# Where the first expert slot takes its memory from, and the order of splits, a routing step and a table around it

## The chip, the cores and the metric

The kernel runs on one core of a Trainium2 chip. The metric is the device time of one execution in microseconds. Before the change three runs gave a median of 810.86 us (810.6 to 813.5). The engines of the core run their own instruction streams in order and wait for each other by semaphores: TensorE (PE), VectorE (DVE), ScalarE (ACT), GpSimd (POOL) and SyncE (SP, which only issues transfers here).

## The reference

Attention with a sigmoid in place of the softmax, and after it a mixture of experts in which every token goes to the one expert with the highest logit:

```python
q, k, v: (8, 12, 448, 64)              # batch, heads, sequence, head dim
scores = matmul(q, k^T) / 8 - log(448)
attn_out = matmul(sigmoid(scores), v)
x = attn_out.transpose(0, 2, 1, 3).reshape(3584, 768)
e_idx = argmax(x @ w_gate, axis=1)     # 8 experts
gate_w = softmax(x @ w_gate)[e_idx];   eom = sigmoid(x @ w_output_gate)
for e in range(8):
    h = maximum(x[e_idx == e] @ w1[e], 0)          # 768 -> 1024
    out[e_idx == e] = gate_w * eom[:, e] * (h @ w2[e])   # 1024 -> 768
```

## The kernel before

**Attention** (`attention`) walks 24 groups of two head pairs. PE multiplies, ACT applies the sigmoid, DVE adds the halves, transposes 32x32 blocks into `xt` (token rows of one batch, two buffers), and after the sixth pair of a batch SP writes `xt` to `x_dram`. Gate logits of four pairs at a time come from `gates`. Per batch, `route` turns logits into a place in one list per expert. It is a generator of steps, "logits", "counts", "places", "rows": after "places" POOL makes `pos`, `den` and others in a chain of small operations, and "rows" begins with DVE's reciprocal of `den` (line 274), after which POOL scatters the list entries.

**Experts.** Tokens of one expert are worked in slots of 256. The first three slots (early) are filled from the first six batches before attention ends; `table(True)` makes the plan of the late slots from all counts, in five parts on DVE, each a step. Each slot (`slot`, line 493) has this work:

- layer 1, eight blocks f of 128 hidden units: twelve matmuls (lines 458, 459) into one of three PSUM banks; then ACT copies half the sum, DVE adds the other (`gl`, line 467), and `high_low` makes the high and low part of block f - 1 in `h` (ACT 471, DVE 472);
- layer 2, four outputs (t, n): 24 matmuls each (lines 484 to 486), the high, low-weight and low-activation products of all eight blocks. ACT evicts y (line 487), POOL scatters rows of y to `out` (line 489).

All numbers are carried as a rounded high part and a low remainder. A split is a cast on ACT (line 424) and a subtraction on DVE (line 425). w2 of a slot is split in four pieces during its layer 1 (`split_w2`, before block 0 and at blocks 1, 3, 5). w1 and the tokens of the next slot are split during layer 2 of this one: three pieces of w1 (`split_w1`), and three of x after `turn_x` has transposed the gathered rows (line 443). POOL gathers the next slot's rows from `x_dram` (line 402, eight gathers), SP loads w1 and w2 only where the expert changes (line 414).

The order on each engine is the order of this code; nothing reorders it. `side()` in `build` is a generator of other work, a step of which runs after each block of layer 1 (not after block 7) and after outputs 1 to 3 of layer 2. It holds the rest of the last batch's routing (`rt`), then the five parts of the late table, then per group of lists the load from DRAM (`load_list`, SP) and, three steps later, the spread over partitions (`spread_lists`: a DVE transpose, line 386, and twelve POOL copies).

Memory of the attention comes from the pool `attn`, which is given back when attention has been issued. `late_memory` then takes its tiles from the same addresses: `h`, `y`, `hb`, `hx`, `w2h`, `w2l`, in this order. A tile there waits for the last reader or writer of what lay at its place, a transfer included.

Of the kernel before, what the change touches and what calls it, by code (L numbers as in the profile page):

```python
# [9 lines left out]
F32 = mybir.dt.float32  # L10
F32R = mybir.dt.float32r
# [3 lines left out]
ALU = mybir.AluOpType  # L15
# [5 lines left out]
B, H, S, D = 8, 12, 448, 64  # L21
NPAIR = H // 2
E = 8
DM = H * D
# [23 lines left out]
def r32(ap):  # L48
    return ap.bitcast(F32)


class Kernel:
# [48 lines left out]
    def late_memory(self):  # L101
        p = self.pool("late")
        self.hs = [p.tile([128, 8, TS], F32R, name=f"h{i}") for i in range(2)]
        self.ys = [p.tile([128, DM], F32, name=f"y{i}") for i in range(2)]
        hb = p.tile([128, DF], F32, name="hb")
        self.hb = hb
        self.hx = p.tile([128, 4, Q4], F32, name="hx")
        self.w2h = p.tile([128, 8, DM], F32R, name="w2h")
        self.w2l = [p.tile([128, 4, DM], F32R, name=f"w2l{i}") for i in range(2)]
        self.lr = [hb[0:32, 192 * i:192 * i + 192] for i in range(5)]  # L110
# [312 lines left out]
    def split(self, raw, hi, lo):  # L423
        self.nc.scalar.copy(hi, raw)  # L424
        self.nc.vector.tensor_tensor(lo, raw, r32(hi), ALU.subtract)  # L425

    def split_w1(self, k):
        self.split(self.w1r[:, 2 * k:2 * k + 2], self.w1p[0][k], self.w1p[1][k])

# [62 lines left out]

    def slot(self, cur, nxt, side=None, begun=False, drain=False):
        nx = self.load_slot(*nxt) if nxt is not None else None
        if drain:
            self.gather(dict(lx=self.lxb[:, 1], xg=self.half_x(1)))
            self.nc.gpsimd.drain()
        self.split_w2(0)
        for f in range(8):
            self.layer1(f, begun and f == 0)  # L500
            if f:
                self.high_low(f - 1)
            if f in (1, 3, 5):
                self.split_w2(f // 2 + 1)
            if side is not None and f < 7:
                next(side, None)
        self.high_low(7)
        self.load_w2(nx)
        self.turn_x(nx)
        self.split_x(nx, 0)  # L510
        self.split_x(nx, 1)
        for i, (t, n) in enumerate(((0, 0), (0, 1), (1, 0), (1, 1))):
            self.layer2(cur, t, n, self.ys[t])
            if i == 0:
                self.split_x(nx, 2)
            if i < 3 and nx is not None:
                self.split_w1(i)
            if side is not None and i > 0:
                next(side, None)
        return nx  # L520
# [59 lines left out]

    def attention(self, pool):
        nc = self.nc
# [3 lines left out]
        t = lambda n, shape: pool.tile(shape, F32, name=n)  # L586
# [6 lines left out]
        xh = t("xh", [128, S])  # L593
        xt = [t(f"xt{i}", [128, S // 32, NPAIR * 32]) for i in range(2)]
        half = [slice(0, 64), slice(64, 128)]
# [78 lines left out]
        for u in range(U * NG + LAG):  # L674
            g, i = divmod(u, U)
# [52 lines left out]
    def build(self, phases="abc"):  # L728
        tc, nc = self.tc, self.nc
# [3 lines left out]
        self.memory()  # L733
        with tc.tile_pool(name="attn", bufs=1) as p:
            rt = self.attention(p)
        self.late_memory()
# [6 lines left out]
        early = lambda k: (self.tab_e, k, self.lts[:, k], self.lxs[:, k], ROWS_E)  # L743
        late = lambda k: (self.tab_l, k, self.lts[:, EARLY + k], self.lxs[:, EARLY + k])

        def side():
# [5 lines left out]
            next(rt)  # L752
            yield
            for _ in rt:
                yield
            yield
            for _ in self.table(True):
# [28 lines left out]
        sd = side()  # L786
        self.mm_ps = self.mm_late
        cur = self.s0
        for k in range(EARLY - 1):
            cur = self.slot(cur, early(k + 1), sd, k == 0)  # L790
        cur = self.slot(cur, late(0), sd)
# [53 lines left out]
```

## Time and profile before

| what | us |
|---|---|
| median of three runs | 810.86 |
| the profiled execution | 810.35 |
| its span | 808.5 |
| PE busy | 788.5 (98%) |
| DVE busy | 503.3 (62%) |
| ACT busy | 490.9 (61%) |
| POOL busy | 311.6 (39%) |

Attention takes the first 282 us; slot 0 begins there with block 0, and slots 1, 2 and 3 begin layer 1 at about 324, 361 and 394 us. After 763 us two half slots of 128 tokens end the kernel. Where PE is at 98%, the only time that another engine can cost is where PE stands still: the timeline of PE shows it in brackets at the instruction after the stand, with the releaser. One bracket further back, the releaser's own timeline tells what that engine had waited for. Spans of POOL are rough.

### The profile page before, as it was taken

The page shows a single profiled execution, that of the slowest core. Times are in us where ns is not written, and L with a number is a line of the kernel's source. Part 1 is how long each engine was busy: PE and PEld are TensorE (multiplying, and loading weights), DVE is VectorE, ACT ScalarE, POOL GpSimd, SP SyncE. Part 2 cuts the span into 40 slices and gives each one's busy share as a digit, 9 for nine tenths or more (in the row PEclk, how much of TensorE's full clock was granted, in tenths as well). Part 3 has the DMA queues.
Part 4 walks back from the last instruction along what each step waited for, and adds up shares of the span by engine and source line. Part 5 has one row for each costly group of instructions (what it writes and reads, how often), then busy time and mean ns, then how long its engine had stood idle before and what let it go on. Part 6 is the DMA issues. An engine that isn't in the chain of part 4 may idle for free. (4 is left out here: it accounts for less than half of the span.)

```text
span 808.5 us, 15212 instructions
## 1 busy us (share of the span) xinstructions
PE 788.5 (98%) x5772; PEld 582.8 (72%) x5772; DVE 503.3 (62%) x731; ACT 490.9 (61%) x665; POOL 311.6 (39%) x454
## 2 busy tenths in 40 slices
PE   9999999999999988999999999999999999999996
PEld 4333333333333378799899999999999999999885
DVE  2344434434457656876767776767767667676696
ACT  5666666666568535464656656665566565665585
POOL 4003302310334565738445144352445523525152
PEclk9999999999999999999999999999999999999999
DMA  6353543525558320236218571192175101758371
GB/s 251 131 206 130 160 192 138 206 87 189 196 181 335 124 103 6 77 111 237 91 40 316 189 267 51 29 332 94 41 257 173 50 39 40 271 160 316 121 299 39
DMA packets 32312, 126.81 MB, mean 157 GB/s; under 512 B 5535, under 2 KB 7823, under 8 KB 28256
## 3 DMA queue, kind: packets, MB, share of 16 engines
q1 hardware_dynamic: 22288, 100.81, 35.1%
q0 software_dynamic: 9936, 24.88, 9.3%
q8 instruction: 50, 0.82, 0.4%
q14 instruction: 38, 0.31, 0.1%
HBM read 153.15 MB, written 23.64 MB: 219 GB/s over the span
## 5 line engine op out<-in xcount | busy, mean ns | idle before, releaser
L458 PE MATMUL ps<-rounded 128*128 128x512 f32 x672 | 236.9, 395 | 4.2 <-DVE gl L467 4.1
L611 ACT ACTIVATE a<-ps,bias_s 128x896 f32<-128x896 f32 x168 | 169.0, 1008 | 97.4 <-PE ps L609 97.4
L459 PE MATMUL ps<-rounded 128*128 128x256 f32 x672 | 189.0, 281 | 1.3 <-DVE rounded L425 1.3
L425 DVE TENSOR_TENSOR rounded<-plain,rounded 128x2048 fp32r<-128x2048 f32 (+3 forms) x107 | 148.9, 1413 | 49.5 <-ACT rounded L424 49.4
L402 POOL DMA_INDIRECT plain<-x_dram,lxs x120 | 149.8, 1248 | 36.6 <-issue 34.8
L486 PE MATMUL ps<-w2h,h 128*128 128x384 f32 x480 | 161.2, 336 | 2.4 <-DVE h L472 1.9
L484 PE MATMUL ps<-w2h,h 128*128 128x384 f32 x480 | 160.8, 335 | 0.3 <-ACT h L471 0.3
L485 PE MATMUL ps<-w2l,h 128*128 128x384 f32 x480 | 160.5, 334 | 0.0
L609 PE MATMUL ps<-kqv 64*64 64x448 f32 x1344 | 158.1, 541 | 0.4 <-ACT a L611 0.4
L618 PE MATMUL ps<-a,kqv 64*64 64x448 f32 x1344 | 157.1, 536 | 0.5 <-ACT pc L260 0.5
L458 PEld LDWEIGHTS ps<-rounded 128*128 128x128 f32 x672 | 126.5, 188 | 34.3 <-DVE gl L467 5.5
L424 ACT CAST rounded<-plain 128x2048 fp32r<-128x2048 f32 (+3 forms) x107 | 124.8, 1199 | 40.8 <-DVE plain L443 40.8
L425 DVE TENSOR_TENSOR w2l<-plain,w2h 128x1536 fp32r<-128x1536 f32 x62 | 108.7, 1758 | 61.1 <-ACT w2h L424 61.1
L459 PEld LDWEIGHTS ps<-rounded 128*128 128x128 f32 x672 | 127.8, 190 | 1.6 <-DVE rounded L425 1.6
L489 POOL DMA_INDIRECT out<-y,lts x28 | 51.2, 1827 | 199.2 <-ACT y L487 131.1
L466 ACT COPY gl<-ps 128x256 f32<-128x256 f32 x112 | 41.7, 373 | 110.1 <-DVE h L472 81.6
L618 PEld LDWEIGHTS ps<-a,kqv 64*64 64x64 f32 x1344 | 51.5, 133 | 76.2 <-issue 74.2
L609 PEld LDWEIGHTS ps<-kqv 64*64 64x64 f32 x1344 | 48.7, 133 | 74.1 <-issue 61.5
L424 ACT CAST w2h<-plain 128x1536 fp32r<-128x1536 f32 x62 | 90.8, 1471 | 11.2 <-DMA x_dram<-xt 8.1
L486 PEld LDWEIGHTS ps<-w2h,h 128*128 128x128 f32 x480 | 90.1, 188 | 4.4 <-DVE h L472 2.4
L484 PEld LDWEIGHTS ps<-w2h,h 128*128 128x128 f32 x480 | 90.1, 188 | 1.7 <-ACT h L471 1.0
L485 PEld LDWEIGHTS ps<-w2l,h 128*128 128x128 f32 x480 | 90.1, 188 | 0.1
(183 smaller groups left out, 563.6 us busy)
## 6 DMA issues: line engine op xcount, KB each, us to landing
plain<-w SPq DMA_DIRECT2D x68, 768.0 KB
plain<-w SPq DMA_DIRECT2D x48, 1024.0 KB
kqv<-kqv SPq DMA_DIRECT2D x23, 1344.0 KB
x_dram<-xt SPq DMA_DIRECT2D x8, 1344.0 KB
plain<-w SPq DMA_DIRECT2D x6, 512.0 KB
plain<-x_dram,lxs POOLq DMA_INDIRECT x120, 3.7
kqv<-kqv SPq DMA_DIRECT2D x1, 896.0 KB
lst<-plain POOLq DMA_DIRECT2D x1, 726.0 KB, 7.5
```

The source lines that it names most:

```text
L402: self.nc.gpsimd.indirect_dma_start(out=s["xg"][:, g], out_offset=None, in_=x4, in_offset=bass.IndirectOffsetOnAxis(ap=s["lx"][:, g:g + 1] ...
L424: self.nc.scalar.copy(hi, raw)
L425: self.nc.vector.tensor_tensor(lo, raw, r32(hi), ALU.subtract)
L458: nc.tensor.matmul(ps, wh[d][:, c], self.xc[:, d].rearrange("p a t -> p (a t)"), start=(d == 0), stop=False)
L459: nc.tensor.matmul(ps[:, 0:TS], wl[d][:, c], self.xc[:, d, 0], start=False, stop=(d == 5))
L484: nc.tensor.matmul(ps, hh[:, f, tk], wh, start=(f == 0), stop=False)
L485: nc.tensor.matmul(ps, hh[:, f, tk], wl, start=False, stop=False)
L486: nc.tensor.matmul(ps, hl[:, f, tk], wh, start=False, stop=(f == 7))
L489: nc.gpsimd.indirect_dma_start(out=self.out, out_offset=bass.IndirectOffsetOnAxis(ap=s["lt"][:, t, 0:1], axis=0), in_=y, in_offset=None, b ...
L609: nc.tensor.matmul(ps[half[h], j, 0:S], kg[half[j], e, 0, o:o + 64], kg[half[j], e, 1], start=True, stop=True)
L611: nc.scalar.activation(at[u % 4], ps[:, :, 0:S], AF.Sigmoid, bias=self.bias_s, scale=1.0 / math.sqrt(D))
L618: nc.tensor.matmul(self.ps_o[e][h][half[j], 0:S], v[half[h], 6 if i == 3 else 3 * e + c, j], a[half[h], j], start=(i in ((0, 3 if h else 4 ...
```

## The change

The rows' tiles `xt` come from a second pool, `rows`. The late tiles are divided: `h`, `w2h` and half of `w2l` from the first pool, the rest, `w2l1`, `y`, `hb`, `hx`, from a pool behind it. In `slot`, w1's first piece is split in two: its cast ahead of `turn_x`, its subtraction behind all three token splits; the other two pieces follow outputs 0 and 1 instead of 1 and 2. In slot 0 a step of `side` runs also after block 7; the routing's "rows" step moves there from block 6, and the table's first part moves from output 2 to output 1 of layer 2. So all later steps come one step sooner.

```diff
     def late_memory(self):
         p = self.pool("late")
         self.hs = [p.tile([128, 8, TS], F32R, name=f"h{i}") for i in range(2)]
+        self.w2h = p.tile([128, 8, DM], F32R, name="w2h")
+        w2l = p.tile([128, 4, DM], F32R, name="w2l0")
+        p = self.pool("later")
+        self.w2l = [w2l, p.tile([128, 4, DM], F32R, name="w2l1")]
         self.ys = [p.tile([128, DM], F32, name=f"y{i}") for i in range(2)]
...
-        self.w2h = p.tile([128, 8, DM], F32R, name="w2h")
-        self.w2l = [p.tile([128, 4, DM], F32R, name=f"w2l{i}") for i in range(2)]
...
+    def high_w1(self, k):
+        self.nc.scalar.copy(self.w1p[0][k], self.w1r[:, 2 * k:2 * k + 2])
+
+    def low_w1(self, k):
+        self.nc.vector.tensor_tensor(self.w1p[1][k], self.w1r[:, 2 * k:2 * k + 2], r32(self.w1p[0][k]), ALU.subtract)
+
     def split_w1(self, k):
-        self.split(self.w1r[:, 2 * k:2 * k + 2], self.w1p[0][k], self.w1p[1][k])
+        self.high_w1(k)
+        self.low_w1(k)
...
-    def slot(self, cur, nxt, side=None, begun=False, drain=False):
+    def slot(self, cur, nxt, side=None, begun=False, drain=False, steps=7):
...
-            if side is not None and f < 7:
+            if side is not None and f < steps:
                 next(side, None)
         self.high_low(7)
         self.load_w2(nx)
-        self.turn_x(nx)
-        self.split_x(nx, 0)
-        self.split_x(nx, 1)
+        if nx is not None:
+            self.high_w1(0)
+            self.turn_x(nx)
+            for k in range(3):
+                self.split_x(nx, k)
+            self.low_w1(0)
         for i, (t, n) in enumerate(((0, 0), (0, 1), (1, 0), (1, 1))):
             self.layer2(cur, t, n, self.ys[t])
-            if i == 0:
-                self.split_x(nx, 2)
-            if i < 3 and nx is not None:
-                self.split_w1(i)
+            if i < 2 and nx is not None:
+                self.split_w1(i + 1)
...
-        xt = [t(f"xt{i}", [128, S // 32, NPAIR * 32]) for i in range(2)]
+        xt = [rows.tile([128, S // 32, NPAIR * 32], F32, name=f"xt{i}") for i in range(2)]
...
-        with tc.tile_pool(name="attn", bufs=1) as p:
-            rt = self.attention(p)
+        with tc.tile_pool(name="attn", bufs=1) as p, tc.tile_pool(name="rows", bufs=1) as q:
+            rt = self.attention(p, q)
...
             yield
             next(rt)
             yield
+            next(rt)
+            yield
+            yield
             for _ in rt:
                 yield
-            yield
             for _ in self.table(True):
                 yield
...
-            cur = self.slot(cur, early(k + 1), sd, k == 0)
+            cur = self.slot(cur, early(k + 1), sd, k == 0, steps=8 if k == 0 else 7)
```

DVE at the end of slot 0's layer 1, before: `gl` is a block's sum, the operation into `h` a block's low half (the last two stand in one row), `den` the routing's.

```order
L261 RECIPROCAL sg<-sg 112x32
L467 TENSOR_TENSOR gl_113<-gl_113,ps 128x256
L472 SCALAR_TENSOR_TENSOR h_2441<-gl_113,h_2440 128x256
L274 RECIPROCAL den<-den 112x4
L467 TENSOR_TENSOR gl_113<-gl_113,ps 128x256
L472 SCALAR_TENSOR_TENSOR h_2441<-gl_113,h_2440 128x256 x2
L443 STREAM_TRANSPOSE plain<-plain 128x8x6x32
```

The same place after:

```order
L263 RECIPROCAL sg<-sg 112x32
L476 TENSOR_TENSOR gl_113<-gl_113,ps 128x256
L481 SCALAR_TENSOR_TENSOR h_2445<-gl_113,h_2444 128x256
L476 TENSOR_TENSOR gl_113<-gl_113,ps 128x256
L481 SCALAR_TENSOR_TENSOR h_2445<-gl_113,h_2444 128x256
L276 RECIPROCAL den<-den 112x4
L481 SCALAR_TENSOR_TENSOR h_2445<-gl_113,h_2444 128x256
L452 STREAM_TRANSPOSE plain<-plain 128x8x6x32
```

The sum of block 7 and the low half of block 6 now stand ahead of the reciprocal of `den`; the low half of block 7 alone stands behind it.

ACT from the end of layer 1 of a slot through its layer 2, before: `rounded` with 128x2x256 is a cast of tokens, with 128x2048 one of w1, `y` an eviction.

```order
L471 ACTIVATE h_2440<-gl_113 128x256 x2
L424 CAST rounded<-plain 128x2x256 x2
L487 ACTIVATE y_2442<-ps,lts 128x384
L424 CAST rounded<-plain 128x2x256
L424 CAST rounded<-plain 128x2048
L487 ACTIVATE y_2442<-ps,lts 128x384
L424 CAST rounded<-plain 128x2048
L487 ACTIVATE y_2443<-ps,lts 128x384
L424 CAST rounded<-plain 128x2048
L487 ACTIVATE y_2443<-ps,lts 128x384
L424 CAST w2h<-plain 128x1536
```

The same place after:

```order
L480 ACTIVATE h_2444<-gl_113 128x256 x2
L430 CAST rounded<-plain 128x2048
L426 CAST rounded<-plain 128x2x256 x3
L496 ACTIVATE y_2452<-ps,lts 128x384
L430 CAST rounded<-plain 128x2048
L496 ACTIVATE y_2452<-ps,lts 128x384
L430 CAST rounded<-plain 128x2048
L496 ACTIVATE y_2453<-ps,lts 128x384 x2
L426 CAST w2h<-plain 128x1536
```

The first cast of w1 has moved from behind the first eviction to ahead of the tokens, the other two by one output each, and the last two evictions follow each other.

## Rows read from the trace of the kernel before

**Rows 1.** The windows view: us; busy (instructions) of PE, PEld, DVE, ACT, POOL; clock, DMA, GB/s.

```profile
290.00:300.00 10.00, 7.66 (x41) 6.57 (x42) 7.38 (x15) 4.84 (x10) 8.01 (x7) 0.83 0.19 52
400.00:700.00 300.00, 300.00 (x1731) 282.10 (x1730) 210.71 (x243) 180.39 (x271) 131.79 (x101) 1.00 0.41 141
```

**Rows 2.** The timeline of PE: start, duration, what [idle before it <- releaser].

```profile
292.34 0.50 PE L458 MATMUL ps<-rounded 128*128 128x512 f32 x1 [2.58 <-DVE gl L467]
...
310.80 0.45 PE L486 MATMUL ps<-w2h,h 128*128 128x384 f32 x1 [1.85 <-DVE h L472]
...
311.43 0.43 PE L486 MATMUL ps<-w2h,h 128*128 128x384 f32 x1
...
331.04 0.50 PE L458 MATMUL ps<-rounded 128*128 128x512 f32 x1 [0.42 <-DVE gl L467]
...
336.55 0.50 PE L458 MATMUL ps<-rounded 128*128 128x512 f32 x1 [1.07 <-DVE gl L467]
...
346.86 0.44 PE L484 MATMUL ps<-w2h,h 128*128 128x384 f32 x1 [0.16 <-ACT h L471]
...
397.09 0.39 PE L459 MATMUL ps<-rounded 128*128 128x256 f32 x1 [1.31 <-DVE rounded L425]
```

**Rows 3.** The timeline of ACT in slot 0.

```profile
288.62 1.47 ACT L424 CAST w2h<-plain 128x1536 fp32r<-128x1536 f32 x1 [8.06 <-DMA x_dram<-xt]
```

**Rows 4.** The timeline of DVE in slot 0.

```profile
284.96 0.63 DVE L657 TENSOR_TENSOR gl<-gl,ps 64x448 f32<-64x448 f32 x1 [1.25 <-PE ps L648]
...
290.13 1.82 DVE L425 TENSOR_TENSOR w2l<-plain,w2h 128x1536 fp32r<-128x1536 f32 x1 [3.92 <-ACT w2h L424]
...
304.87 1.76 DVE L425 TENSOR_TENSOR w2l<-plain,w2h 128x1536 fp32r<-128x1536 f32 x1 [0.93 <-ACT w2h L424]
...
309.93 0.18 DVE L274 RECIPROCAL den<-den 112x4 f32<-112x4 f32 x1 [2.43 <-POOL den L270]
...
310.33 1.03 DVE L472 SCALAR_TENSOR_TENSOR h<-gl,h 128x256 fp32r<-128x256 f32 x2
```

**Rows 5.** The timeline of POOL in slot 0.

```profile
290.16 0.99 POOL L402 DMA_INDIRECT plain<-x_dram,lxs  x1 [0.16 <-issue]
...
294.33 2.38 POOL L402 DMA_INDIRECT plain<-x_dram,lxs  x1 [0.30 <-issue]
...
300.78 2.06 POOL L402 DMA_INDIRECT plain<-x_dram,lxs  x1 [0.30 <-issue]
305.07 1.67 POOL L262 TENSOR_TENSOR pos<-pc,off 112x32 f32<-112x32 f32 x1 [2.23 <-ACT pc L260]
```

**Rows 6.** The timeline of DVE from slot 0 to slot 1.

```profile
322.67 2.29 DVE L425 TENSOR_TENSOR rounded<-plain,rounded 128x2048 fp32r<-128x2048 f32 x1 [1.04 <-ACT rounded L424]
...
336.09 0.40 DVE L467 TENSOR_TENSOR gl<-gl,ps 128x256 f32<-128x256 f32 x1
...
336.76 0.15 DVE L356 TENSOR_SCALAR hb<-hb 1x15 f32<-1x15 f32 x1
...
337.72 0.40 DVE L366 CAST tbil<-hb 1x24 int32<-1x24 f32 x1
...
345.95 0.52 DVE L386 STREAM_TRANSPOSE lt<-hb 32x192 f32<-32x192 f32 x1
```

**Rows 7.** The timeline of DVE at the end of slot 2.

```profile
384.39 1.78 DVE L443 STREAM_TRANSPOSE plain<-plain 128x1536 f32<-128x1536 f32 x1 [3.28 <-DMA plain<-x_dram,lxs]
386.86 1.29 DVE L425 TENSOR_TENSOR rounded<-plain,rounded 128x512 fp32r<-128x512 f32 x2 [0.69 <-ACT rounded L424]
...
390.18 6.86 DVE L425 TENSOR_TENSOR rounded<-plain,rounded 128x2048 fp32r<-128x2048 f32 x3 [1.12 <-ACT rounded L424]
```

**Rows 8.** The timeline of ACT in the last full slot.

```profile
747.75 0.42 ACT L471 ACTIVATE h<-gl 128x256 fp32r<-128x256 f32 x1 [0.17 <-DVE gl L467]
...
751.91 2.42 ACT L424 CAST rounded<-plain 128x512 fp32r<-128x512 f32 x2
```

**Rows 9.** The timeline of SP's transfers in the last full slot.

```profile
729.53 0.37 SPq L414 DMA_DIRECT2D plain<-w  x1
```

More of the change, by code (lines that the diff above doesn't have):

```diff
@@ L579, in half_slot, with attention @@
             self.split_w1_row(5)
-    def attention(self, pool):
+    def attention(self, pool, rows):
         nc = self.nc
```

## The prediction

> **What bounds the kernel now.** I read the windows view first, for where TensorE loses time at all. From 400 to 700 us PE is busy for 300.00 of 300 us at full clock [rows 1]: the full slots are bound by TensorE's own work, and no edit to the order of other engines gains there. The timeline of PE then gives the losses before 400 us that the change can reach: its first matmul after each idle stretch carries that stretch and its releaser in brackets [rows 2]. They are 2.58 us at block 3 of slot 0, 1.85 us at block 6's low half in layer 2, 0.42 and 1.07 us in slot 1's layer 1, 0.16 us at its layer 2, and 1.31 us at the start of slot 3, where a low half of w1 is missing. Third, the timelines of ACT, DVE and POOL at these places tell who was late: the reader is to follow each bracket back one engine further.
>
> Slot 0: the first w2 cast on ACT waited 8.06 us for the write of token rows to DRAM [rows 3], and so the DVE split behind it began at 290.13 [rows 4]. Both sums (h of blocks 0 and 1) stand behind that split on DVE, and PE stops for want of a PSUM bank. At the end of layer 1 DVE stood 2.43 us before the reciprocal of `den`, which POOL makes [rows 4], and blocks 6 and 7 stand behind it.
>
> **Part 1, token rows in their own pool.** The cast no longer waits for the write. What it waits for next is the end of the attention's other readers: the gates' matmuls on PE, which end just before DVE's 284.96 [rows 4], whose wait of 1.25 us they end. ACT is free then (the cast's wait began at 288.62 - 8.06 = 280.56). So the cast starts near 284.96 instead of 288.62, 3.66 us sooner, and the split ends at 291.95 - 3.66 = 288.29. The first sum follows within 0.4 us (the same operation takes 0.40 in [rows 6]), at 288.7; PE asks at 292.34 - 2.58 = 289.76. The 2.58 us go, and with them the clock loss that followed: 0.83 over 290 to 300 us [rows 1], a mean of full-speed 2.4 GHz and about a third of the stretch at 1.2 GHz. But layer 1 of slot 0 has four w2 splits, four casts and routing between its sums, a chain on ACT and DVE that PE caught up with in the old trace. PE therefore cannot gain more than that chain moves: 3.66 us up to block 6, not 2.58 + 1.7 for the clock.
>
> **Part 2, the reciprocal behind block 7.** It now stands behind block 6's low half and before block 7's. PE stops one block later, at the matmul that began at 311.43 [rows 2]. When it can go is POOL's affair, and POOL does not move by 3.66 us: its eight gathers begin at 290.16, tied to list writes that the change leaves alone, and the last ended at 300.78 + 2.06 = 302.84 [rows 5]. The first place operation (`pos`) waited 2.23 us after them for ACT's copy, which the chain now brings 3.66 us sooner, to about 301.1. So POOL begins it at 302.9 when the gathers are done. It took 1.67 us because DVE's fourth split ran from 304.87 to 306.63 [rows 4, 5]; that split now ends at 302.97, so `pos` ends at 303.1 to 303.5. From its end at 306.74 to the reciprocal at 309.93 were 3.19 us: the reciprocal comes at 306.3 to 306.7. Two of the gathers took 2.38 and 2.06 us against 0.99 for the first [rows 5]; one more such stretch adds 1.4 us, to 308.1. If POOL gained nothing at all, it stays at 309.93. I take 306.7, next to the row with the gathers' old end. Reciprocal 0.18 and block 7's low half (0.5 of the 1.03 for two, [rows 4]) put PE's matmul at 307.4 instead of 311.43: **4.0 us gained**. PE could be there at 311.43 - 1.85 - 3.66 = 305.92, so 1.5 us of waiting remain. Ends of this term: 0.8 us (reciprocal at 309.93, matmul at 310.6) and 4.4 us (reciprocal at 306.3).
>
> On that lock the Trainium skill (SBUF — State Buffer, section "SBUF: two separate sides") says that a VectorE instruction with two SBUF inputs and a GpSimd instruction exclude each other for the whole instruction, whichever starts first. `pos` agrees, at 1.67 us; the gather at 290.16 does not, at 0.99 us beside a split that had begun at 290.13. By the strict rule the splits, now 3.66 us earlier, hold other gathers, and the sum would be 1.4 us worse; I take the trace's mixture.
>
> **Part 3, the table a step sooner, splits one output sooner.** Slot 2 shows the new split order's worth: turn at 384.39, first token split at 386.86, three of these about 2.0 us, then the three w1 lows 6.86 us without a gap, 395.7; before, the lows began at 390.18 and ended at 397.04 [rows 7]. The first high cast of w1 now fills ACT's wait for the turn, so the lows can follow the tokens at once. PE wanted the last at 397.09 - 1.31 = 395.78: **1.31 us gained**, with nothing to spare from this edit alone; but the list for that slot is also spread before the last output's scatter on POOL, so gathers and turn come sooner too. Bounds 0 and 1.31.
>
> Slot 1: with block 7's low half done at 307.35, the same 11.3 us end the lows at 318.65. Before they ended at 322.67 + 2.29 = 324.96, and the third sum at 336.09 + 0.40 = 336.49 [rows 6]: 11.53 us of table, splits and sums. Now the table's last part, 336.76 to about 337.8, also stands before that sum: 12.6 us, so 331.25. PE without its two waits and 4.0 us sooner wants it at 336.55 - 1.49 - 4.0 = 331.06. It waits about 0.25 us instead of 1.49: **1.25 us gained** (bounds 0 and 1.49). Against that, the spread of the first list (DVE, 0.52 us at 345.95) now stands ahead of block 6's sum, on the chain whose wait was 0.16 us [rows 2, 6]: **0.45 us lost** (bounds 0 and 0.5).
>
> Two reorderings I cost at nothing. One scatter of outputs goes behind twelve small POOL copies, but its buffer is next written a slot later. The evictions of y stand behind more casts; three banks cover that. If that cover went, the rows of 400 to 700 us would show waits.
>
> **Sum.** 4.0 + 1.31 + 1.25 - 0.45 = 6.1 us. The profiled execution took 810.35 us (span 808.5), which is 0.5 below the median of 810.86. 810.35 - 6.1 = 804.25; with part of that half microsecond I forecast **804.5 us**, its own range 803.3 to 806.2.
>
> **Rivals.**
> - *POOL stays where it was* (more gathers held by splits that moved under them). The reciprocal comes at 309.93 or so, PE waits 4.7 us at block 7, part 2 gains 0.8: 810.35 - 0.8 - 1.31 - 1.25 + 0.45 = 807.4. A wait that long may bring the slow clock back: 0.17 of 10 us, 809.1. For it: two held gathers in eight. Against it: `pos` itself waited 2.23 us on ACT, a wait that goes.
> - *The pool does not free the cast*: another attention tile or the write itself holds it through a second wait. Then slot 0 keeps its 2.58 us, only the reciprocal's move and the later parts count, again about 807.4. Against it: the cast's old wait is explained by that write alone.
> - *All waits go*: POOL catches up and every gap of [rows 2] with the clock's 1.7 us closes: 7.4 + 1.7 = 9.1, so 801.3. The chain argument speaks against it.
> - *Slower*: w1's first high cast stands at the head of ACT right behind block 7, at 748.2 in the last full slot instead of behind the row at 751.91 [rows 8]. ACT runs in order; if the load of w1 has not landed, tokens, evictions and splits all stand behind it. The slack is about 3.6 us before PE feels it in the next slot; from there each microsecond costs one in each of some 12 slots: 1 us late makes 804.5 + 12 = 816. Against it: the third load was issued at 729.53 [rows 9], 18.6 us ahead of that cast, and the loads are issued sooner now.
>
> **How the numbers follow.** Forecast 0.68, POOL stays 0.10, cast not freed 0.10, all waits go 0.07, slower 0.05. The range 803.0 to 807.8 holds the first and most of the next two, about 0.83 in all. Half a per cent, about what a measurement of this kernel can tell, is 4.05 us: faster means below 806.8. That is 0.93 of the forecast, a quarter of the next two and all of the fourth: 0.75. Slower 0.05, the rest 0.20.
>
> **What would show it.** Right: the first w2 cast at about 285, no PE wait at block 3, full clock from 290 to 300; a PE wait of 1 to 2 us at block 7's low half, ended by DVE behind the reciprocal; 0.2 to 0.3 us at block 5 of slot 1; about 0.6 us at block 6 of its layer 2; none near 395; and 400 to 700 us unchanged. Wrong: the cast still ended by a DMA, POOL's `pos` later than 304, or ACT waiting for a load of w1.

## The result, and the profile after

The changed kernel took 802.81 us (median of six runs, 801.64 to 803.18), the kernel before in the same comparison 810.73 (six runs, 808.87 to 813.5): ratio 0.9897, 95% interval 0.9878 to 0.9915. The forecast was 804.5 with a range from 803.0: the sign is right, but 7.9 us were gained where 6.4 were forecast, and the median lies just below the range. Three more comparisons gave the same ratio: 0.9901 [0.9876, 0.9927], 0.9890 [0.9865, 0.9915] and 0.9885 [0.9866, 0.9904].

The windows of the changed kernel (columns as in [rows 1]):

```profile
290.00:300.00 10.00, 9.90 (x62) 8.27 (x61) 7.21 (x16) 4.91 (x12) 7.87 (x8) 1.00 0.24 59
306.00:308.00 2.00, 1.84 (x6) 1.84 (x7) 1.79 (x2) 0.26 (x2) 1.21 (x5) 0.57 0.03 8
308.00:310.00 2.00, 2.00 (x9) 2.00 (x8) 1.52 (x3) 2.00 (x5) 0.57 (x2) 0.57 0.02 1
400.00:700.00 300.00, 300.00 (x1732) 282.24 (x1732) 208.19 (x244) 180.01 (x271) 133.24 (x98) 1.00 0.43 147
```

The 10 us behind 290 have PE busy for 9.90 us at full clock (before 7.66 at 0.83), and the full slots are as they were. New is a clock of 0.57 from 306 to 310. The timeline of PE shows what is left of [rows 2] up to slot 3:

```profile
303.76 0.44 PE L493 MATMUL ps<-w2h,h 128*128 128x384 f32 x1 [0.33 <-ACT h L480]
...
306.16 0.59 PE L495 MATMUL ps<-w2h,h 128*128 128x384 f32 x1 [1.13 <-DVE h L481]
...
340.91 0.44 PE L493 MATMUL ps<-w2h,h 128*128 128x384 f32 x1 [0.33 <-ACT h L480]
...
390.00 0.38 PE L468 MATMUL ps<-rounded 128*128 128x256 f32 x1 [0.16 <-DVE rounded L433]
```

No stop at block 3 of slot 0; 1.13 us at block 7's low half; no stop in slot 1's layer 1 (0.15 to 0.18 us at block 5 in the three later profiles, where 0.2 to 0.3 was forecast); 0.16 at slot 3 where 1.31 stood. ACT, DVE and POOL of the changed kernel show why [rows 3 to 5]:

```profile
284.11 1.48 ACT L426 CAST w2h<-plain 128x1536 fp32r<-128x1536 f32 x1 [4.44 <-PE ps L658]
```
```profile
284.06 0.62 DVE L667 TENSOR_TENSOR gl<-gl,ps 64x448 f32<-64x448 f32 x1 [1.25 <-PE ps L658]
...
289.57 1.76 DVE L427 TENSOR_TENSOR w2l<-plain,w2h 128x1536 fp32r<-128x1536 f32 x1 [0.95 <-ACT w2h L426]
...
295.69 1.76 DVE L427 TENSOR_TENSOR w2l<-plain,w2h 128x1536 fp32r<-128x1536 f32 x1 [0.93 <-ACT w2h L426]
...
300.30 1.76 DVE L427 TENSOR_TENSOR w2l<-plain,w2h 128x1536 fp32r<-128x1536 f32 x1 [0.93 <-ACT w2h L426]
...
305.61 0.18 DVE L276 RECIPROCAL den<-den 112x4 f32<-112x4 f32 x1 [1.44 <-POOL den L272]
305.71 0.39 DVE L481 SCALAR_TENSOR_TENSOR h<-gl,h 128x256 fp32r<-128x256 f32 x1
306.02 1.77 DVE L452 STREAM_TRANSPOSE plain<-plain 128x1536 f32<-128x1536 f32 x1
```
```profile
290.55 1.61 POOL L404 DMA_INDIRECT plain<-x_dram,lxs  x1 [0.30 <-issue]
...
296.21 2.06 POOL L404 DMA_INDIRECT plain<-x_dram,lxs  x1 [0.30 <-issue]
...
299.82 0.95 POOL L404 DMA_INDIRECT plain<-x_dram,lxs  x1 [0.30 <-issue]
300.79 1.38 POOL L264 TENSOR_TENSOR pos<-pc,off 112x32 f32<-112x32 f32 x1
```

The cast is released by the gates' matmuls, not by a DMA. The reciprocal still waits for POOL, but only block 7's low half stands behind it. In slots 1 and 2 DVE of the changed kernel [rows 6, 7] has:

```profile
329.73 0.40 DVE L476 TENSOR_TENSOR gl<-gl,ps 128x256 f32<-128x256 f32 x1
...
338.92 0.52 DVE L388 STREAM_TRANSPOSE lt<-hb 32x192 f32<-32x192 f32 x1
...
378.98 1.78 DVE L452 STREAM_TRANSPOSE plain<-plain 128x1536 f32<-128x1536 f32 x1 [3.81 <-DMA plain<-x_dram,lxs]
381.45 1.90 DVE L427 TENSOR_TENSOR rounded<-plain,rounded 128x512 fp32r<-128x512 f32 x3 [0.69 <-ACT rounded L426]
383.26 6.69 DVE L433 TENSOR_TENSOR rounded<-plain,rounded 128x2048 fp32r<-128x2048 f32 x3
```

The sum that stood at 336.09 behind the table came at 329.73, the spread of the list now stands ahead of block 6's sum at 339.38, and the low halves of w1 follow the tokens with no gap.

**A ledger by stages.** Brackets alone do not add up to what a stage loses, and attention does not always end at the same time. So I count each profile from the start of the last gate add on DVE (284.96 in [rows 4], 284.06 above), and take as a stage's start its first matmul: PE goes from `w2h, h` to `rounded` at the start of a layer 1, and back at its end. In the third profile of the changed kernel, where the gate add began at 283.67, slot 1's layer 1 reads so on PE's timeline:

```profile
318.36 0.33 PE L495 MATMUL ps<-w2h,h 128*128 128x384 f32 x1
318.53 0.39 PE L467 MATMUL ps<-rounded 128*128 128x512 f32 x1
...
335.94 0.28 PE L468 MATMUL ps<-rounded 128*128 128x256 f32 x1
336.06 0.34 PE L493 MATMUL ps<-w2h,h 128*128 128x384 f32 x1
```

It begins at 318.53 - 283.67 = 34.86 and takes 336.06 - 318.53 = 17.53. All numbers below are us behind that add, or lengths; the repeats belong to the experiments.

| profile | turn of x for slot 1 | slot 1 begins | its layer 1 | its layer 2 | slot 3's layer 1 | end of span |
|---|---|---|---|---|---|---|
| before | 26.32 | 39.25 | 19.17 | 17.32 | 18.49 | 523.54 |
| before, again | 26.31 | 40.68 | 19.19 | 17.31 | 18.77 | 525.00 |
| changed | 21.96 | 36.42 | 16.64 | 17.66 | 17.08 | 516.94 |
| changed, 2nd | 21.96 | 34.86 | 17.57 | 17.76 | 17.25 | 516.44 |
| changed, 3rd | 21.95 | 34.86 | 17.53 | 17.79 | 17.08 | 516.03 |
| changed, 4th | 21.94 | 34.86 | 17.51 | 17.81 | 17.03 | 516.55 |

A layer 1 without a stop takes 16.64 us (slot 2 in every profile), so the kernel before lost 2.53 us in slot 1's layer 1, where its brackets sum to 1.49, and 1.85 in slot 3's, where one bracket says 1.31.

### The profile page after: what moved, and what is told of

It reads as the page before. It is cut to its first block, busy times and chain, and to the rows that moved or that the text cites. A ratio compares the mean times of both kernels' runs of the same rounds, so it can differ in the third digit from the quotient of the medians.

```text
span 801.0 us, 15186 instructions
## 1 busy us (share of the span) xinstructions
PE 787.2 (98%) x5772; PEld 582.9 (73%) x5772; DVE 498.7 (62%) x731; ACT 490.7 (61%) x665; POOL 308.4 (39%) x454
## 5 line engine op out<-in xcount | busy, mean ns | idle before, releaser
L404 POOL DMA_INDIRECT plain<-x_dram,lxs x120 | 147.0, 1225 | 37.7 <-issue 34.3
L498 POOL DMA_INDIRECT out<-y,lts x28 | 55.9, 1995 | 194.4 <-ACT y L496 118.7
L433 DVE TENSOR_TENSOR rounded<-plain,rounded 128x2048 fp32r<-128x2048 f32 x46 | 102.9, 2285 | 2.2 <-ACT rounded L430 2.2
L430 ACT CAST rounded<-plain 128x2048 fp32r<-128x2048 f32 x46 | 87.6, 1904 | 0.0
```

Of the source, the lines that this page charges most:

```text
L404: self.nc.gpsimd.indirect_dma_start(out=s["xg"][:, g], out_offset=None, in_=x4, in_offset=bass.IndirectOffsetOnAxis(ap=s["lx"][:, g:g + 1] ...
L433: self.nc.vector.tensor_tensor(self.w1p[1][k], self.w1r[:, 2 * k:2 * k + 2], r32(self.w1p[0][k]), ALU.subtract)
```

## The experiments

All medians are set against runs of the kernel before on the same chip.

| run | median (range, n) | ratio [95%] | slot 1 begins, its layer 1, end |
|---|---|---|---|
| pools alone | 808.05 (805.86 to 809.97, 12) | 0.9962 [0.9943, 0.9981] | 37.11, 19.16, 521.6 |
| routing step and table alone | 811.42 (809.62 to 813.76, 12) | 1.0009 [0.9990, 1.0028] | 38.57, 19.12, 526.8 |
| split order alone | 806.55 (804.81 to 810.68, 9) | 0.9948 [0.9925, 0.9972] | 40.62, 16.84, 520.7 |
| change without pools | 805.80 (805.41 to 806.48, 6) | 0.9926 [0.9909, 0.9943] | 38.56, 17.52, 520.2 |
| change without routing step | 802.55 (800.91 to 803.7, 6) | 0.9880 [0.9862, 0.9898] | 37.10, 16.83, 517.1 |
| reciprocal behind block 7 | 802.55 (802.06 to 802.97, 6) | 0.9884 [0.9867, 0.9901] | 33.50, 19.00, 516.7 |
| `den` first | 803.17 (800.44 to 804.28, 6) | 0.9890 [0.9869, 0.9911] | 33.60, 17.46, 515.1 |
| `den` first, again | 802.53 (799.91 to 803.37, 6) | 0.9885 [0.9858, 0.9911] | 33.57, 17.48, 514.9 |
| added memset | 802.82 (802.08 to 805.71, 6) | 0.9899 [0.9872, 0.9925] | 35.64, 17.56, 517.1 |
| `den` first, old routing step | 804.74 (804.37 to 806.65, 5) | 0.9858 [0.9839, 0.9876] | 34.09, 16.88, 514.2 |
| changed, beside the last | 807.58 (806.26 to 808.77, 5) | 0.9885 [0.9866, 0.9904] | 34.86, 17.51, 516.6 |

**The parts alone.** Each is one part of the diff put on the kernel before. The pools:

```diff
...
-        xt = [t(f"xt{i}", [128, S // 32, NPAIR * 32]) for i in range(2)]
+        xt = [rows.tile([128, S // 32, NPAIR * 32], F32, name=f"xt{i}") for i in range(2)]
...
```

> Only the pools are divided as in the change; split order, routing step and table are as before. Main theory (the three parts work on different stops and the routing chain caps the first): the first w2 cast is released by the gates' matmuls 3.7 us sooner, the stop at block 3 goes, but block 6's low half still stands behind the reciprocal of den, so PE stands there about 1.5 to 2.5 us, the clock falls for some 3 us, and the stops of 0.4, 1.1 and 1.3 us in slots 1 and 3 stay: about 2 us faster than before, 808 to 809.5. Rival (the pools alone are nearly the whole change): 803 to 804.5. Rival (attention itself became 0.9 us shorter through the moved tiles): DVE's last gate copy begins near 284.1 here as in the changed kernel, against 285.0 before.

Measured 0.9962. The stop at block 3 is gone, slot 0's chain comes 3.7 us sooner, but the ledger gains only about half of it (523.54 to 521.6). The timeline of PE and the windows of this run:

```profile
307.17 0.45 PE L488 MATMUL ps<-w2h,h 128*128 128x384 f32 x1 [1.85 <-DVE h L474]
```
```profile
308.00:310.00 2.00, 2.00 (x7) 2.00 (x8) 1.41 (x1) 0.55 (x2) 1.00 (x1) 0.50 0.05 9
310.00:312.00 2.00, 2.00 (x10) 2.00 (x9) 1.69 (x3) 2.00 (x5) 0.64 (x1) 0.69 0.00 0
```

Behind the stop of 1.85 us, which [rows 2] has too, PE now runs at 1.2 GHz for over 3 us. In the profile of before it did not; in the second one of before (under the repeats) it did, so this is not the pools' doing. Against that second profile the pools gain 3.4 us.

The routing step and the table:

```diff
-            if side is not None and f < 7:
+            if side is not None and f < steps:
...
+            next(rt)
+            yield
+            yield
             for _ in rt:
                 yield
-            yield
```

> Only the routing's last step and the table are moved as in the change; pools and split order are as before. Main theory: block 3's stop of 2.6 us stays, block 6 is no longer held, block 7 is, about 1 us less lost there; the table's parts now stand ahead of the sums of slot 1 without the splits having come sooner, so block 3 and block 5 of slot 1 wait 2 to 3 us together instead of 1.5; the stop at slot 3 shrinks. In all 0 to 1.5 us faster than before, 809 to 811. Rival (each part is worth its own term of the sum, added up): 0.8 + 1.2 us, 808.5 or less.

Measured no change. Slot 0's stop shrinks to 1.14 us, but slot 3, whose stop was expected to shrink, now stops twice and its layer 1 takes 21.88 us instead of 18.49. The timelines of DVE and PE in this run show why:

```profile
390.58 4.57 DVE L425 TENSOR_TENSOR rounded<-plain,rounded 128x2048 fp32r<-128x2048 f32 x2 [1.12 <-ACT rounded L424]
395.07 0.50 DVE L386 STREAM_TRANSPOSE lt<-hb 32x192 f32<-32x192 f32 x1
395.51 2.24 DVE L425 TENSOR_TENSOR rounded<-plain,rounded 128x2048 fp32r<-128x2048 f32 x1
```
```profile
395.21 0.39 PE L459 MATMUL ps<-rounded 128*128 128x256 f32 x1 [1.24 <-DVE rounded L425]
397.80 0.38 PE L459 MATMUL ps<-rounded 128*128 128x256 f32 x1 [1.63 <-DVE rounded L425]
```

With the table a step sooner a list's transpose stands ahead of the last low half of w1, for which PE waits 1.63 us more. In the new split order all three low halves stand ahead of it.

The split order:

```diff
-        self.turn_x(nx)
-        self.split_x(nx, 0)
-        self.split_x(nx, 1)
+            self.high_w1(0)
+            self.turn_x(nx)
+            for k in range(3):
+                self.split_x(nx, k)
+            self.low_w1(0)
...
```

> Only the order of the next slot's splits is changed; pools, routing step and table are as before. Main theory: slot 0's stops at blocks 3 and 6 stay as they were; w1's lows end about 2.3 us sooner before slot 1, which takes away both of its layer 1 stops (0.42 and 1.07) and the 1.31 us before slot 3; each stop is worth some 0.27 us more than its bracket because the matmul pipeline drains and refills: 3.0 to 3.8 us faster, about 807.3. Rival (brackets are the whole price): 2.8 us. Rival (the slack was there and PE stands elsewhere): under 1 us.

Measured 0.9948, 4.2 us, a little more than the 3.0 to 3.8 expected: slot 1's layer 1 shrinks from 19.17 to 16.84 and slot 3's to 16.64.

**All but one part.** The change without the pools:

> Changed kernel without the new pools: the w2 cast again waits for the write of token rows. Theory A (the parts add up): the routing step alone measured +0.7 us and the split order alone -4.2, so 810.7 - 3.5 = 807.2. Theory B (the routing step costs something only as long as w1's three low halves stand late on DVE, and in the new split order it is a gain): below 806.5, about 805.5, with one PE wait of about 1 us at block 7 of slot 0 instead of 1.85 at block 6, none of 1 us in slot 1's layer 1 and none at slot 3. By both the stop of about 2.6 us at block 3 of slot 0 is back.

Measured 805.80 and 0.9926: theory B. The routing step, worth nothing alone, lowers the ratio from 0.9948 to 0.9926 behind the new split order, though these two intervals overlap. The stop of 2.63 us at block 3 is back. And the change without the routing step:

> Changed kernel with the routing step and the late table in their old places (pools and split order kept). Theory A (parts add up): 810.7 - 2.7 - 4.2 = 803.8. Theory B (the routing step is worth what it takes off the wait at block 6, 1.85 against 1.13, plus the spread that it puts ahead of a scatter): 803.5 to 804.5. A rival, that the gain of the routing step is eaten by the table that stands ahead of slot 1's sums: 802.9 or less, the same as the changed kernel. Expected in the profile: the wait of 1.85 us at block 6's low half of slot 0 again, no stop in slot 1's layer 1.

Measured 0.9880 beside 0.9885 to 0.9901 for the whole change: the rival of my expectation, no difference that can be told. The ledger says why: without the step slot 1 begins 2.2 us later (the stop is 1.85 us, and the slow clock follows), but its layer 1 is 0.7 and its layer 2 0.4 us shorter, and slot 3's layer 1 0.4. What remains is 0.8 us (517.1 against 516.3), which the medians cannot tell; how much of it the slow clock of this one profile makes stays open.

**The wait at block 7.** First the reciprocal put behind block 7's low half:

```diff
-            if side is not None and f < steps:
+            if side is not None and f < 7:
                 next(side, None)
         self.high_low(7)
+        if side is not None and steps == 8:
+            next(side, None)
```

> Changed kernel with the reciprocal of den behind block 7's low half on DVE instead of ahead of it. The PE wait of 1.13 us at block 7 of slot 0 goes (with about 0.27 that each stop costs beyond its bracket), and no slow clock can follow it. Theory A (slot 1 is set by DVE's chain that begins at the turn of x, which the reciprocal still holds): PE comes 1.4 us sooner to slot 1 and waits there about 1.2 us more at blocks 3 and 5; net 0.2 to 0.5 us below the changed kernel, about 802.4. Theory B (a PE stop is worth itself, the chain has room): 1.4 us below the changed kernel, about 801.4, with no stops above 0.5 us in slot 1.

Measured 802.55, ratio 0.9884; the wait is gone and slot 1 begins 1.4 us sooner, and then PE of this run gives it all back:

```profile
324.73 0.50 PE L467 MATMUL ps<-rounded 128*128 128x512 f32 x1 [0.72 <-DVE gl L476]
...
329.78 0.50 PE L467 MATMUL ps<-rounded 128*128 128x512 f32 x1 [0.55 <-DVE gl L476]
...
334.39 0.50 PE L467 MATMUL ps<-rounded 128*128 128x512 f32 x1 [0.17 <-DVE gl L476]
```

Slot 1 begins at 33.50 and its layer 1 ends at 52.50; in the changed kernel it began at 34.86 and ended at 52.4. Theory A by its mechanism, though its gain of 0.2 to 0.5 us is not seen (516.7 against 516.3): DVE's chain from the turn of x sets the end of slot 1's layer 1. Three brackets of 1.44 us together made the stage 2.36 us longer than 16.64.

Then POOL's sums for `den` ahead of those for `pos`:

```diff
+        tt(sg[:, 0], sg[:, 0], sg[:, 1], ALU.mult)
+        self.sum8(sg[:, 0], R["den"])
+        tt(R["den"], R["den"], self.eps, ALU.add)
         tt(R["pos"], R["pc"][0:CP, 0:NCH * E].rearrange("p (c e) -> p c e", e=E),
...
-        tt(sg[:, 0], sg[:, 0], sg[:, 1], ALU.mult)
-        self.sum8(sg[:, 0], R["den"])
-        tt(R["den"], R["den"], self.eps, ALU.add)
```

> Changed kernel with POOL's sums for den ahead of its sums for pos. The reciprocal comes 1.4 to 1.9 us sooner, so the wait of 1.13 us at block 7 of slot 0 goes and the turn of x comes about 1.2 us sooner with it. Theory A (slot 1 is set by the chain from the turn): 1.2 to 1.5 us below the changed kernel, about 801.4, since chain and PE move together; Theory B (POOL's order does not set the reciprocal): 802.8, the wait stays. A rival: the list rows of the last batch come later by the wait of POOL for the reciprocal of the sigmoid (up to 1.5 us), and slots that read the list wait: no gain.

> POOL's sums for den ahead of those for pos, again, beside the changed kernel on the same chip. Theory A (chain and PE move together, stops at block 7 and slot 3 gone): 515.1 us from the last gate add to the end as before, 1.2 to 1.8 below the changed kernel, and its median 1 to 2 us below it. Theory B (the first result's median, 803.17, is the truth): no difference to the changed kernel.

In both profiles DVE no longer waits at the reciprocal (here the second):

```profile
303.84 0.17 DVE L276 RECIPROCAL den<-den 112x4 f32<-112x4 f32 x1
...
304.45 1.78 DVE L452 STREAM_TRANSPOSE plain<-plain 128x1536 f32<-128x1536 f32 x1
```

The turn comes at 20.71 instead of 21.95, and slot 1's layer 1 ends at 51.05 instead of 52.39: chain and PE move together, the span behind the gate add is 1.2 to 1.5 us shorter, as theory A expects, though the stop at slot 3 stays (its layer 1 takes 17.06 and 17.14 us). The medians do not show it: 802.53 against 802.47 for the changed kernel beside it, with runs from 799.91 to 803.37. The profiles support A; as a time the gain is not shown.

Last a memset in front of block 7's low half, which lengthens the wait:

```diff
                 next(side, None)
+                if f == 7:
+                    self.nc.vector.memset(self.ys[0], 0.0)
```

> Changed kernel with a memset of one 128x768 tile on DVE between the reciprocal of den and block 7's low half in slot 0, so that the wait there grows from 1.13 us by the memset's length, an estimated 0.4 to 0.8 us. Theory A (slot 1 is set by DVE's chain from the turn of x, which the memset moves by its length too): the time grows by that length alone, 0.4 to 0.8 us, whether or not the clock falls behind the wait. Theory B (a wait and the slow clock after it add up): by the length and another 1.6 us if the clock falls. Waits of 1.85 us and more brought 1.2 GHz in all profiles but one, so a fall is expected at 1.6 us or more.

The timelines of DVE and of PE in this run:

```profile
305.45 0.18 DVE L276 RECIPROCAL den<-den 112x4 f32<-112x4 f32 x1 [1.44 <-POOL den L272]
305.73 0.70 DVE L517 MEMSET y<- 128x768 f32 x1
```
```profile
306.76 0.45 PE L495 MATMUL ps<-w2h,h 128*128 128x384 f32 x1 [1.92 <-DVE h L481]
```

The memset took 0.70 us and the wait became 1.92. Slot 1 begins 0.78 us later, its layer 1 ends 0.8 later (53.20), the median is 0.35 above the changed kernel beside it, inside the uncertainty. The stages agree with theory A; but the fall of the clock that I expected did not come (1.00 from 300 to 320 us), and without it theory B forecasts the same, so this run does not part the two. It does show that the length of the wait does not decide the clock by itself.

**Repeats.** The changed kernel three times more and the kernel before once more:

> The changed kernel once more, for its spread and for attention's part. Main theory: 802 to 803.5, with DVE's last gate copy anywhere between 284 and 285, as chance of a gather's landing has it. Rival (the 0.9 us belong to the change): 284.1 again, while the kernels that leave the pools as before show 285.0.

> The changed kernel again, as the base for the two beside it: 802 to 804. Whether its wait at block 7 of slot 0 (1.13 us so far) is followed by 1.2 GHz is open: one of two profiles so far showed it. By the theory that the gates' end and not the clock makes most of the spread, the time from the last gate add to the end is 516.4 to 517.0 us again.

> The kernel before, profiled again: the forecast stands on one profile of it. By the theory that the attention part scatters by chance, the last gate add comes between 283.4 and 285.0 and not always at 284.96, and the time from it to the end is 523 to 524 us again; by the rival, that the old kernel's attention part is slower, it comes at 284.9 or later.

The 1.13 us wait brought the slow clock in the first profile only. Second to fourth show 1.00 behind it; here the third:

```profile
308.00:310.00 2.00, 2.00 (x13) 2.00 (x12) 1.92 (x4) 2.00 (x5) 0.57 (x2) 1.00 0.02 1
```

In the second profile of before the stop of 1.84 us did bring it (the timeline of PE and the windows):

```profile
310.43 0.57 PE L486 MATMUL ps<-w2h,h 128*128 128x384 f32 x1 [1.84 <-DVE h L472]
```
```profile
310.00:312.00 2.00, 1.57 (x5) 1.57 (x6) 1.86 (x4) 0.42 (x1) 1.26 (x5) 0.65 0.00 0
312.00:314.00 2.00, 2.00 (x8) 2.00 (x7) 1.31 (x3) 1.30 (x3) 0.55 (x1) 0.50 0.05 10
```

Slot 1 then began 1.43 us later, and that stayed to the end (525.00 against 523.54). The slow clock of 292 to 298 us was missing there, and the stop at block 6 came at 25.83 us behind the gate add as in the first profile (25.84): that earlier slow stretch cost nothing. As to the gates' end, before had 284.96 and 284.60, the changed kernel 284.06, 283.36 and 283.67, but the new pools alone 285.00 and the old pools with the new split order 284.04: it is no effect of the pools. The kept traces show two places where it arises, neither in the order of work that the edit changes. DVE's first transpose into `xt` begins anywhere from 14.20 to 15.70 us; from there to the forty-fifth every profile but the two of the third chip (the runs lie on three) takes 250.8 to 250.9 us; and from that to the forty-seventh it is 12.55 to 13.33. One thing speaks against pure chance: without those two, the five profiles with the routing step in its old place have the gate add at 284.04 to 285.00, the nine with it moved at 283.36 to 284.19 (on the third chip 288.51 and 287.95). What ties the two stays open.

**Pace of the table, and a faster kernel.** `den` first, new pools and new split order, but routing step and table in their old places:

```diff
...
-            next(rt)
-            yield
-            yield
             for _ in rt:
                 yield
+            yield
             for _ in self.table(True):
...
```

> New pools, new split order and POOL's sums for den ahead of those for pos, but the routing step and the late table at their old places. The reciprocal should no longer wait, so block 6 and 7 of slot 0 have no stop of over 0.5 us and slot 1 begins at 33.6 us behind the last gate add, as with the new routing step. Theory A (layer 1 of slot 1 ends a fixed 30.4 us behind the turn of x whatever the table's pace): it ends at 51.1 to 51.6, and the time is that of the kernel with den first, 1.0 to 1.5 us below the changed kernel. Theory B (it is the table a step sooner that makes slot 1 stop): layer 1 of slot 1 takes 16.7 us without a stop and ends at 50.4, its layer 2 takes 17.36 instead of 17.8, and the time is 2.0 to 2.8 us below the changed kernel.

> The changed kernel beside it on the same chip: 801.5 to 804, 516.0 to 517.0 us from the last gate add to the end; layer 1 of slot 1 ends 30.4 us behind the turn of x unless the clock fell at block 7.

DVE's two operations of slot 0 in the kernel with `den` first and the old pace, and PE's stops in its slots 0 and 1:

```profile
308.39 0.18 DVE L276 RECIPROCAL den<-den 112x4 f32<-112x4 f32 x1 [0.95 <-POOL den L266]
...
309.73 1.78 DVE L452 STREAM_TRANSPOSE plain<-plain 128x1536 f32<-128x1536 f32 x1
```
```profile
308.26 0.44 PE L493 MATMUL ps<-w2h,h 128*128 128x384 f32 x1 [0.33 <-ACT h L480]
309.26 0.44 PE L495 MATMUL ps<-w2h,h 128*128 128x384 f32 x1 [0.38 <-DVE h L481]
342.97 0.44 PE L493 MATMUL ps<-w2h,h 128*128 128x384 f32 x1 [0.17 <-ACT h L480]
```

Nearer to theory B, not all of it: DVE still waits 0.95 us at the reciprocal, so slot 1 begins 0.5 us later than with `den` first alone (34.09). Its layer 1 takes 16.88 us, but ends at 50.97 where B had 50.4. That is 29.75 us behind the turn of x, not theory A's 30.4: with the table and the lists a step sooner the chain is at least 0.6 us longer. Slot 1's layer 2 takes 17.33 us and slot 3's layer 1 16.64, each 0.4 to 0.5 less than with `den` first alone. This kernel took 804.74 us against 807.58 for the changed kernel on the same chip (the changed kernel is 4.8 us longer there than in its first comparison; attention ended later, the last gate add at 288.51 and 287.95). The ratios 0.9858 and 0.9885 have intervals that just overlap, the ledgers differ by 2.4 us: faster than both kernels by its median and its stages.

## Why the prediction came out too high

**Part 1 held.** The cast began at 284.11 (forecast near 284.96; the gates ended 0.9 us sooner in this profile), block 3 does not stop, 290 to 300 us is at full clock. The claim that the slow clock there cost nothing beside the chain is shown by the two profiles of before.

**Part 2 held, a little low.** Block 7's matmul came 22.10 us behind the gate add instead of 26.47: 4.37 us gained, forecast 4.0. The wait was 1.13 us, forecast 1 to 2. The gathers ended at 300.77, 16.7 us behind the gate add instead of 17.9 [rows 5], so `pos` did not have to wait for them until 302.9 as I had it. That gained nothing: `pos` ended 0.11 us behind the fourth split, at 302.17, as it had before, and 18.1 us behind the gate add is the lower end of what I forecast for it.

The "mixture" of held and free gathers was a misreading. The gathers at 290.55 and 296.21 began inside the splits at 289.57 and 295.69 and ended 0.82 to 0.83 us behind the ends of these; the other six began inside no split and took 0.94 to 0.99 us. The kernel before had three such, not two: 1.32, 2.38 and 2.06 us. The rule of the Trainium skill (SBUF — State Buffer, section "SBUF: two separate sides"), which it states for GpSimd operations that read SBUF, lets whichever of the two starts first keep the other out. The trace agrees where the split starts first, but for the gather at 290.16 of the kernel before, 0.03 us behind a split's start; where the gather did, as at 299.82, the split at 300.30 still took 1.76 us like the others. So fewer gathers were held after the splits had moved, and not more as I had feared.

**Part 3 is the step that failed: it took a stop's bracket for its whole price.** "1.25 us gained" in slot 1's layer 1 measured 1.6 (19.17 to 17.5, where no slow clock came before it), and "1.31 us gained" at slot 3 measured 1.4 in the changed kernel's 17.08, with 0.44 still lost behind a bracket of 0.16. A stop costs something at both ends that the bracket leaves out. PE of the kernel before at block 5 of slot 1 shows it:

```profile
335.19 0.28 PE L459 MATMUL ps<-rounded 128*128 128x256 f32 x1
336.55 0.50 PE L458 MATMUL ps<-rounded 128*128 128x512 f32 x1 [1.07 <-DVE gl L467]
336.88 0.28 PE L459 MATMUL ps<-rounded 128*128 128x256 f32 x1
```

The last matmul counts as work for its 0.28 us, though undisturbed the next one begins 0.12 us behind its start: 0.16 us. The first one behind the stop is followed after 0.33 us instead of 0.24: 0.09 us. By stages it is more: three brackets of 1.44 us cost 2.36, one of 1.31 cost 1.85, one of 0.16 cost 0.44, so some 0.3 to 0.5 us each beyond the bracket, of which these rows show 0.25. The kernel before even had one that no bracket shows: two starts of matmuls from 340.77 us on come 0.36 us later together than their neighbours' pitch. "0.45 us lost" in slot 1's layer 2 is right: 17.32 to 17.66 to 17.81. The gathers for slot 3 did not gain as I had said: the turn waits for a DMA at 378.98 as before, 24.2 us behind the start of slot 2's layer 1 instead of 23.7, and the stop is small because the low halves follow without gaps. "With nothing to spare" was right: 0.15 to 0.33 us of the stop are left.

With stages instead of brackets the sum is 4.4 + 1.6 - 0.45 + 1.4 = 7.0. The profiles without the slow clock at blocks 6 and 7 differ by 523.54 - 516.34 = 7.2 (the mean of the changed kernel's 2nd to 4th). So the mechanisms were right and the terms about 0.9 us too small together: part 2 by 0.4, part 3 by 0.5.

**The base was one profile.** The stop of 1.84 or 1.85 us at block 6 was followed by 1.2 GHz in four of five profiles that have it (second of before, pools alone, split order alone, change without routing step), but not in the one that the forecast stood on; the wait of 1.13 or 1.14 us in one of six. Its price is 1.4 us where nothing covers it (before) and 0.6 us in the changed kernel, where slot 1 then has no stop (16.64) and layer 1 ends at 53.06 instead of 52.4. The timed runs have no trace, but each has its mean granted clock on record, and the times go with it: of the 26 runs of before beside the pools alone, seven at 0.996 average 808.9 us and fourteen at 0.992 to 0.994 average 812.5; the profile that the forecast stood on had 0.996. Of the changed kernel's six runs the two at 0.998 took 801.64 and 802.02 us, the four at 0.996 took 802.80 to 803.18.

**What put the time below the range.** The profiles of before and after, 810.35 and 802.80 us, differ by 7.55: 6.60 behind the gate add, where 6.1 was forecast, and 0.90 ahead of it, which no term of the forecast contains. With the quarter of a microsecond that I put on 804.25 that makes up the 1.7 us from 804.5 to 802.81. So more than half of the miss is the gates' end, and the 0.2 us by which the time lies below 803.0 are less than its scatter. How the medians' 7.9 us divide between stages, clock and gates' end stays open.

**The rivals.** POOL did not stay, the pool freed the cast, and no load of w1 was late. ACT of the changed kernel in the last full slot, where [rows 8] stood, begins w1's high cast with no wait in brackets:

```profile
740.71 1.90 ACT L430 CAST rounded<-plain 128x2048 fp32r<-128x2048 f32 x1
```

"All waits go", the fastest rival at 801.3, came nearest in time, but waits did stay. The argument against it, that DVE's chain limits PE, was right, and stronger than I used it: with the new split order and the new routing step slot 1's layer 1 ended 30.3 to 30.5 us behind the turn of x in eight of nine profiles, whatever PE waited before (in the first of the changed kernel PE came so late behind the slow clock that it was 31.1). That is also why the gain of the routing step was forecast as part of 4.0 us and turned out as nothing that the medians tell: 0.8 us by the ledger here, and a loss of 0.7 to 0.9 us where `den` comes first (514.9 and 515.1 against 514.2). It begins slot 1 sooner and puts the table where slot 1 has to wait for it.

## What to carry to other kernels

Price a stop by the length of its stage against an undisturbed one, not by the bracket; and count from an event just ahead of the change, so that what scatters before it falls out. A step moved ahead on one queue is paid for by what it then stands ahead of a slot later: undo each part of a change against the whole, not only against the kernel before, since a part can cost alone what it does not cost beside the others (slot 3's layer 1 took 21.88 us with the routing step alone, 17.1 in the whole). The medians alone would not show it: the single gains of 2.7, nothing and 4.2 us come to 6.9 against 7.9, inside their uncertainty.

## What was not expected of the hardware

The clock behind a stop is not settled by the stop's length: 1.13 us brought 1.2 GHz (0.57 from 306 to 310 us) in one profile and 1.00 in the next of the same kernel; 1.92 us brought none, 1.84 and 1.85 us brought it four times of five, 2.56 us once not, 2.55 to 2.67 us in the four other profiles that have the stop at block 3.

A gather that POOL starts while DVE splits a piece of w2 is held until that split ends. In all sixteen profiles, of slot 1's eight gathers those that began 0.2 to 1.3 us behind the start of a split of w2 ended 0.81 to 0.83 us behind its end and took 1.32 to 2.38 us; all others took 0.94 to 0.99, among them those that began within 0.03 us of a split's start. A split that began during a gather was not held: 1.76 us each time.
